# A turned down product in the first MoE, six buffers for the last evictions, and block 0 with whole rows of v

## The chip, the core and the metric

The kernel runs on one core of a Trainium2 chip. Its time is the device time of one execution, in microseconds (us), and smaller is better. Four engines matter: TensorE (PE, with PEld for its weight loads), VectorE (DVE), ScalarE (ACT) and SyncE (SP), which issues all transfers; GpSimd (POOL) does little. The engines run their own instruction lists in order and wait for each other through semaphores.

## What is computed

A linear attention, whose heads are put side by side as 512 features of 2304 tokens, and two MLPs of 512 x 2048 x 512 (called MoE) behind it, all in float32:

```python
q_s = softmax(q, axis=-1)            # over the 64 features of a head
k_s = softmax(k, axis=2)             # over the 576 positions of a sequence
kv = np.einsum('bhsd,bhse->bhde', k_s, v)
x = np.einsum('bhsd,bhde->bhse', q_s, kv)     # (4, 8, 576, 64) -> (2304, 512)
h = x @ w_in;  y = softplus(h) @ w_out        # first MoE
h = y @ w2_in; out = elu(h) @ w2_out          # second MoE
```

## The kernel before

Tokens are cut into six blocks of 384 (t = 0 to 5), and two blocks form a pair (p = 0, 1, 2, called pairs 1 to 3). The 2048 features of an MLP are cut into eight quads of 256 (f = 0 to 7). The kernel goes through 48 quads: MoE m, pair p, quad f.

A quad has an **up product** and a **down product**. The up product (`add_up`) makes 256 features for 768 tokens by a Strassen-like scheme of seven products of 6 matmuls each, 128 x 128 weights against 384 columns, into the two PSUM banks of the ring "ha"; sums and the nonlinearity follow on ScalarE and VectorE. Float32 is imitated with three matmuls in the rounded type fp32r: each operand is split into a high part (gh) and a low part (gl), and high x high, high x low and low x high are added. The first two quads of the first pair use plain f32 instead (`direct`).

The down product (`add_down`) adds the quad to six PSUM banks `acc` (half, r), each 128 tokens x 512 features, that stay open for all eight quads of a pair. There, g is the stationary operand (128 tokens) and w_out the moving one (512 columns): 12 steps of 3 matmuls. Steps of the down product of one quad stand between the up products of the next. After the last quad of a pair, `add_store` copies the six banks to SBUF tiles y (a ring of two buffers), alternating between ScalarE and VectorE, and stores them: to DRAM tiles yd in the first MoE, to the output in the second.

The second MoE needs its input with features on the partitions. `add_y` (L522 to L539) loads each yd tile, turns it on TensorE by four 128 x 128 transposes into a bank of "ha" (py, L528), and ScalarE copies it into sx. The load is released five quads ahead of the pair. `add_forms` makes the operands xf from sx.

The attention runs block by block, in head pairs hp. `add_k` loads k and v, finds the maximum of k over positions (L316, a transpose on TensorE, L327, and a spread by TensorE), subtracts it (L342), takes the exponential (L350, ScalarE) and makes k x v with an additional column of ones (pk, L359); the sums' reciprocal (L368, L372) scales it into the block-diagonal kvbd (L379, ScalarE). v is loaded into rows with one free column per 64 features (L309), so in pieces of 256 bytes. `add_q` takes the softmax of q. For the first two head pairs of blocks 0 and 1 the exponential takes each group of 64 columns in an activation of its own, with the maximum as its bias and the sum as its accumulator (L431); elsewhere VectorE subtracts (L437), one activation follows (L443), and VectorE sums (L447). q is transposed (pq, L482), copied (xq, L488), multiplied by kvbd (px, L498) and copied into sx (L511). Only then can the first up product run (L878).

The order of all instructions is computed by the class `Plan`: a list scheduler that has a duration for every step, a due date for the steps of TensorE, and for each engine takes the step that can start and is due first. The attribute `early` moves a group's due dates forward, and a step that opens a tile waits until its ring has a free buffer. What the scheduler gives is the fixed order in which each engine, SyncE's queue included, runs its list.

## Time and profile before

| | us |
|---|---|
| median of 3 runs | 869.89 |
| lowest and highest run | 867.58, 870.22 |
| the profiled execution | 870.18 |
| its span, first to last instruction | 868.4 |
| TensorE busy in it | 838.6 |

A line of the timeline gives the start and the duration of one instruction, or of several in a row (xN) from the first start to the last end; matmuls are pipelined, so the distance of two starts is what one costs, and its duration contains its way through the array. What ended an engine's idle time stands behind "<-". In the names, `acc<-wo_o,gh` means: writes acc, reads wo_o and gh.

### The profile page before, as it was taken

What the parts mean: (1) busy time and instruction counts of PE and PEld (TensorE: products, weight loads), DVE (VectorE), ACT (ScalarE), POOL (GpSimd) and SP (SyncE); (2) the same over time, 40 slices, a digit from 0 to 9 for tenths busy, and PEclk for the clock granted to TensorE, in tenths of its full rate; (3) what the DMA queues carried; (4) which work ended last, traced back from release to release, by engine and by line L of the source; (5) the groups of instructions that cost most, each with busy time, mean ns of one, the idle gap of its engine ahead of it and who ended that gap; (6) DMA issues with size and microseconds to landing.
All of it is one profiled execution on the core that took longest, in us unless ns stands there. A gap on an engine that the chain in (4) does not pass through costs nothing.

```text
span 868.4 us, 11687 instructions
## 1 busy us (share of the span) xinstructions
PE 838.6 (97%) x4570; PEld 724.9 (83%) x4570; DVE 566.1 (65%) x812; ACT 532.3 (61%) x819; POOL 2.8 (0%) x24
## 2 busy tenths in 40 slices
PE   3889999999999999999999999999999999999996
PEld 2555888888988888988988988899888888888895
DVE  7676887666888779577668677767543446543433
ACT  4777788675686877665566665666534455534433
POOL 0000000000000000000000000000000000000000
PEclk9799999999999999999999999999999999999999
DMA  9868675514987627667664777784664563663521
GB/s 247 241 186 271 236 263 192 146 74 157 279 289 239 212 102 246 242 240 268 236 215 192 284 279 289 281 288 185 218 244 168 190 254 138 237 235 135 208 107 73
DMA packets 66774, 186.35 MB, mean 215 GB/s; under 512 B 22688, under 2 KB 28832, under 8 KB 57760
## 3 DMA queue, kind: packets, MB, share of 16 engines
q1 hardware_dynamic: 66720, 185.61, 61.8%
q8 instruction: 36, 0.59, 0.3%
q14 instruction: 18, 0.15, 0.1%
HBM read 131.07 MB, written 54.53 MB: 214 GB/s over the span
## 4 chain that ended last, share of the span: by engine, by line
PE 88%; ACT 6%; DVE 3%; DMA 1%; issue 1%; SPq 0%; ACTq 0%; DVEq 0%
PE acc L1008 42%; PE ub L817 19%; PE uc L817 9%; PE up L899 5%; PE ua L817 5%; PE acc L1003 2%; PE px L498 2%; PE up L878 1%; ACT q L431 1%; PE py L528 1%; ACT L920 1%; PE pk L359 1%; ACT raw_i L628 1%; DMA k<-in_k_dram 1%; PE pq L482 1%
## 5 line engine op out<-in xcount | busy, mean ns | idle before, releaser
L1008 PE MATMUL acc<-wo_o,gh 128*128 128x512 f32 x1104 | 350.3, 398 | 0.0
L1008 PEld LDWEIGHTS acc<-wo_o,gh 128*128 128x128 f32 x1104 | 201.0, 188 | 28.1 <-issue 0.5
L1008 PE MATMUL acc<-wo_o,gl 128*128 128x512 f32 x552 | 218.5, 396 | 0.1
L817 PE MATMUL ub<-xf,wf_i 128*128 128x384 f32 x960 | 194.9, 337 | 0.0
L817 PEld LDWEIGHTS ub<-xf,wf_i 128*128 128x128 f32 x960 | 172.0, 188 | 13.8 <-ACT s L830 0.6
L851 DVE TENSOR_TENSOR h<-uc,s 128x384 f32<-128x384 f32 x80 | 44.4, 555 | 141.2 <-PE uc L817 129.7
L830 ACT COPY s<-ub 128x384 f32<-128x384 f32 x120 | 57.4, 478 | 111.4 <-PE ub L817 111.1
L1008 PEld LDWEIGHTS acc<-wo_o,gl 128*128 128x128 f32 x552 | 103.4, 187 | 22.8 <-DVE gl L973 0.5
L973 DVE TENSOR_TENSOR gl<-g,gh 128x768 fp32r<-128x768 f32 x92 | 87.8, 954 | 26.5 <-ACT gh L969 26.3
L969 ACT CAST gh<-g 128x768 fp32r<-128x768 f32 x92 | 76.9, 836 | 37.5 <-DVE g L960 36.7
L817 PE MATMUL uc<-xf,wf_i 128*128 128x384 f32 x480 | 97.5, 337 | 0.2 <-ACT g L920 0.2
L817 PEld LDWEIGHTS uc<-xf,wf_i 128*128 128x128 f32 x480 | 85.7, 188 | 7.3 <-DVE h L851 0.9
L899 PE MATMUL up<-xf,wp 128*128 128x384 f32 x288 | 57.0, 344 | 0.9 <-ACT g L920 0.9
L899 PEld LDWEIGHTS up<-xf,wp 128*128 128x128 f32 x288 | 50.5, 188 | 6.4 <-issue 2.1
L817 PE MATMUL ua<-xf,wf_i 128*128 128x384 f32 x240 | 48.2, 335 | 0.1
L960 DVE SCALAR_TENSOR_TENSOR g<-h,u 128x768 f32<-128x768 f32 x48 | 45.9, 956 | 1.2
L817 PEld LDWEIGHTS ua<-xf,wf_i 128*128 128x128 f32 x240 | 42.5, 188 | 0.9 <-DVE h L851 0.6
L948 ACT ACTIVATE u<-h 128x768 f32<-128x768 f32 x48 | 40.6, 845 | 3.8 <-DVE h L851 2.4
L952 ACT ACTIVATE u<-u 128x768 f32<-128x768 f32 x48 | 40.6, 847 | 1.2
L836 ACT COPY h<-ub 128x384 f32<-128x384 f32 x24 | 11.5, 480 | 44.5 <-PE ub L817 44.5
L956 DVE TENSOR_SCALAR u<-u 128x768 f32<-128x768 f32 x48 | 26.7, 555 | 16.3 <-ACT u L952 16.2
L733 ACT CAST wf_i<-r_i 128x512 fp32r<-128x512 f32 (+1 forms) x48 | 23.7, 511 | 17.6 <-PE uc L817 16.6
(90 smaller groups left out, 907.3 us busy)
## 6 DMA issues: line engine op xcount, KB each, us to landing
wo_o<-wod SPq DMA_DIRECT2D x30, 1024.0 KB, 6.8
wf_i<-wfd SPq DMA_DIRECT2D x16, 1792.0 KB, 7.3
raw_i<-in_moe_w_in_dram SPq DMA_DIRECT2D x16, 1024.0 KB, 6.5
raw_o<-in_moe_w_out_dram SPq DMA_DIRECT2D x16, 1024.0 KB, 5.9
wod<-wo_o SPq DMA_DIRECT2D x16, 1024.0 KB, 5.9
wfd<-wf_i SPq DMA_DIRECT2D x8, 1792.0 KB, 9.1
r_i<-w32i SPq DMA_DIRECT2D x24, 512.0 KB, 4.5
w32i<-ti_i SPq DMA_DIRECT2D x14, 512.0 KB, 5.0
```

What stands on the lines that cost most here:

```text
L733: nc.scalar.copy(view(0, lo, n, c), get())
L817: nc.tensor.matmul(ps[:, :BLK], T[wk][:, lo : lo + P], T[xk][:, (2 * c + kc) * BLK : (2 * c + kc + 1) * BLK], start=(i in first and kc == ...
L830: nc.scalar.copy(new(sk), T[key][:, :BLK])
L851: nc.vector.tensor_tensor(T[hk][:, half * BLK : (half + 1) * BLK], T[key][:, :BLK], T[sk], op=ALU.add)
L899: nc.tensor.matmul(ps[:, :BLK], T[wk[a]][:, lo : lo + P], T[xk][:, (2 * c + kc) * BLK : (2 * c + kc + 1) * BLK], start=(n_ == 0 and kc == ...
L948: nc.scalar.activation(new(uk), T[hk], AF.Relu, scale=-1.0)
L952: nc.scalar.activation(T[uk], T[uk], AF.Exp, scale=-1.0)
L956: nc.vector.tensor_scalar(T[uk], T[uk], -1.0, None, op0=ALU.add)
L960: nc.vector.scalar_tensor_tensor(new(gk), T[hk], 0.0, T[uk], op0=ALU.max, op1=ALU.add)
L969: nc.scalar.copy(new(hk), T[gk])
L973: nc.vector.tensor_tensor(new(lk), T[gk], T[hk].bitcast(F32), op=ALU.subtract)
L1008: nc.tensor.matmul(ps, T[g][:, col : col + P], T[wk][:, (2 * a + j) * DM : (2 * a + j + 1) * DM], start=(first and n == 0), stop=(f == NQ ...
```

## The change

1. In the first MoE the down product of pairs 2 and 3 is **turned** (`turned(m, p)`, `add_down_turned`): w_out is now the stationary operand (128 features) and g the moving one (768 tokens). The 768 tokens don't fit a bank of 512 columns, so for each of four groups of features (kc) the first 512 tokens go to a bank of their own, and the last 256 of two groups share a bank: six banks as before. A quad has 8 steps of 6 matmuls, alternating between 512 and 256 columns. `add_store` evicts these six banks and stores them in a DRAM tile with features on the partitions, and `add_y` loads a block of it straight into sx; transposes and copies out of PSUM remain for pair 1 alone.
2. The six evictions at the very end use three rings (y, yl, raw), two buffers each, and get due dates one after the other; the last tile is evicted in two halves, by VectorE and ScalarE.
3. In block 0 each head pair's v is loaded as whole rows of 2304 bytes into a staging tile vr, and ScalarE copies it into v; kvbd is made by VectorE. The activations of 64 columns (L431) are gone; blocks 0 and 1 go the way of the others.
4. The scheduler starts with ScalarE's table set "exp" as loaded, takes TensorE's early steps as 1.1 instead of 2.2 times as long, and has other values of `early`.

```diff
-        lock, table = 0.0, None
+        lock, table = 0.0, "exp"
...
-                dur *= 2.2
+                dur *= PE_EARLY
...
+PE_EARLY = 1.1
...
-        @step(DMA, n * t_dma(2 * P * C * D * 4), w=[vk], after=LAT)
-        def _():
-            for g, hp in enumerate(hps):
-                nc.sync.dma_start(
-                    out=vt()[:, g, :, :D],
-                    in_=v[b, 2 * hp : 2 * hp + 2].rearrange("h (p c) d -> (h p) c d", c=C),
-                )
+        vsrc = lambda hp: v[b, 2 * hp : 2 * hp + 2].rearrange("h (p c) d -> (h p) c d", c=C)
+        if early:
+            vr = ("vr", b, hps[0])
+            @step(DMA, t_dma(P * C * D * 4), make=[(vr, "xf")], after=LAT, behind=[kload[b, hps[0]]])
+            def _():
+                T[vr] = new(vr, F32)[:, : C * D].rearrange("p (c d) -> p c d", c=C)
+                nc.sync.dma_start(out=T[vr], in_=vsrc(hps[0]))
+            @step(ACT, t_act(C * D), r=[vr], w=[vk])
+            def _():
+                nc.scalar.copy(vt()[:, 0, :, :D], T[vr])
...
-        @step(ACT, 0.5 * n, r=[pk, rs], w=[("kvbd", b % 2, hp) for hp in hps])
+        eng = DVE if early else ACT
+        @step(eng, (0.28 if early else 0.5) * n, r=[pk, rs], w=[("kvbd", b % 2, hp) for hp in hps])
         def _():
             for g, hp in enumerate(hps):
                 for j in range(2):
                     rows = slice(64 * j, 64 * j + 64)
-                    nc.scalar.activation(
-                        kvbd[b % 2, hp][rows, rows], pkv()[rows, g, :D], AF.Copy, scale=T[rs][rows, g : g + 1]
-                    )
+                    o, i, f = kvbd[b % 2, hp][rows, rows], pkv()[rows, g, :D], T[rs][rows, g : g + 1]
+                    if eng == DVE:
+                        nc.vector.tensor_scalar(o, i, f, None, op0=ALU.mult)
+                    else:
+                        nc.scalar.activation(o, i, AF.Copy, scale=f)
...
-        if t < 2 and hps[0] < 2:
-            @step(DVE, 0.072, w=[qm])
-            def _():
-                nc.vector.tensor_scalar(T[qm][:, :N], T[qm][:, :N], -1.0, None, op0=ALU.mult)
-            @step(ACT, N * 0.24, r=[qm], w=[qk], make=[(qd, "qd")], tab="exp")
-            def _():
-                new(qd)
-                for j in range(N):
-                    nc.scalar.activation(
-                        flat()[:, j], flat()[:, j], AF.Exp, bias=T[qm][:, j], accum_out=T[qd][:, j]
-                    )
...
+        @step(DVE, t_dve(n), r=[qm], w=[qk])
+        def _():
+            nc.vector.tensor_tensor(
+                flat(), flat(), T[qm][:, :N].to_broadcast([P, N, D]), op=ALU.subtract
+            )
+        @step(ACT, t_act(n), w=[qk], tab="exp")
+        def _():
+            nc.scalar.activation(flat(), flat(), AF.Exp)
+        @step(DVE, t_dve(n), r=[qk], make=[(qd, "qd")])
+        def _():
+            nc.vector.tensor_reduce(new(qd)[:, :N], flat(), axis=AX.X, op=ALU.add)
...
+        if turned(0, t // 2):
+            p, lo = t // 2, t % 2 * BLK
+            @step(
+                DMA, t_dma(P * KC * BLK * 4), r=[("ytd", p, i) for i in range(2 * R)], make=[(xk, "sx")],
+                w=[("xs", 1, t, kc) for kc in range(KC)], after=LAT, behind=behind,
+            )
+            def _():
+                nc.sync.dma_start(
+                    out=new(xk).rearrange("p (k c) -> p k c", k=KC),
+                    in_=T["yd", p].rearrange("p (k c) -> p k c", k=KC)[:, :, lo : lo + BLK],
+                )
+            return
...
+    turned = lambda m, p: m == 0 and p > 0
+    def add_down_turned(m, p, f, wk, t0):
+        for n, (j, kc) in enumerate((j, kc) for j in range(2) for kc in range(KC)):
+            hk, lk = ("gh", m, p, f, j), ("gl", m, p, f, j)
+            keys = [("acc", m, p, kc), ("acc", m, p, KC + kc // 2)]
+            first = f == 0 and j == 0
+            made = keys[: 1 if kc % 2 else 2] if first else []
+            @step(
+                PE, 1.5 * DN, w=[key for key in keys if key not in made], r=[hk, lk, ("woh", m, f), ("wol", m, f)],
+                hold=[wk], make=[(key, f"acc{kc // 2}") for key in made], due=t0 + (2 + n) * UP + 1.5 * n * DN + 0.01,
+                line=("acc", kc),
+            )
+            def _(j=j, kc=kc, hk=hk, lk=lk, keys=keys, made=made, first=first):
+                for key in made:
+                    new(key)
+                parts = [
+                    (T[keys[0]], slice(0, 512), True),
+                    (T[keys[1]][:, kc % 2 * 256 : kc % 2 * 256 + 256], slice(512, 2 * BLK), kc % 2 == 0),
+                ]
+                for n, (g, a) in enumerate(((hk, 0), (hk, 1), (lk, 0))):
+                    lo = (2 * a + j) * DM + kc * P
+                    for ps, cols, starts in parts:
+                        nc.tensor.matmul(
+                            ps, T[wk][:, lo : lo + P], T[g][:, cols],
+                            start=(first and n == 0 and starts), stop=(f == NQ - 1 and j == 1 and n == 2),
+                            skip_group_check=True,
+                        )
...
+        if turned(m, p):
+            return add_down_turned(m, p, f, wk, t0)
...
+        if turned(m, p):
+            T["yd", p] = dp.tile([P, KC * 2 * BLK], F32, name=f"yd{p}")
+            to = T["yd", p].rearrange("p (k c) -> p k c", k=KC)
+            for i, n in enumerate((0, 4, 1, 2, 5, 3)):
+                ak, sk = ("acc", m, p, n), ("yt", m, p, n)
+                eng = DVE if i % 2 else ACT
+                @step(eng, t_act(DM, True) if eng == ACT else t_dve(DM), r=[ak], make=[(sk, "y")], due=after_quad(m, p, NQ - 1) + SLOT)
+                def _(eng=eng, ak=ak, sk=sk):
+                    (nc.scalar.copy if eng == ACT else nc.vector.tensor_copy)(new(sk), T[ak])
+                @step(DMA, t_dma(P * DM * 4), r=[sk], w=[("ytd", p, n)], after=LAT)
+                def _(n=n, sk=sk):
+                    if n < KC:
+                        nc.sync.dma_start(out=to[:, n, :512], in_=T[sk])
+                    else:
+                        lo = 2 * (n - KC)
+                        nc.sync.dma_start(
+                            out=to[:, lo : lo + 2, 512:], in_=T[sk].rearrange("p (k c) -> p k c", k=2)
+                        )
+            return
...
+                final = (m, p) == (1, NPAIR - 1)
+                ring = ("y", "yl", "raw")[(R * half + r) // 2] if final else "y"
+                both = final and (half, r) == (1, R - 1)
+                for n_, eng in enumerate((DVE, ACT) if both else (eng,)):
+                    n = DM // 2 if both else DM
+                    @step(
+                        eng, t_act(n, True) if eng == ACT else t_dve(n), r=[ak],
+                        w=[("y2", m)] if n_ else [], hold=[sk] if n_ else [], make=[] if n_ else [(sk, ring)],
+                        due=after_quad(m, p, NQ - 1) + SLOT + (R * half + r if final else 0), line="y2" if both else None,
+                    )
+                    def _(eng=eng, ak=ak, sk=sk, n_=n_, n=n):
+                        if not n_:
+                            T[sk] = new(sk, F32)[:, :DM]
+                        cols = slice(n_ * n, n_ * n + n)
+                        (nc.scalar.copy if eng == ACT else nc.vector.tensor_copy)(T[sk][:, cols], T[ak][:, cols])
...
-    ATT = ((70.0, 50.0), (35.0, 20.0))
+    ATT = ((120.0, 50.0), (50.0, 10.0))
...
-        early(6.0 if i else 200.0)
+        early(4.0 if i else 200.0)
...
-        early((180.0, 30.0, 0.0)[min(f, 2)] if plain(m, p) else 10.0)
+        early((150.0, 10.0, 0.0)[min(f, 2)] if plain(m, p) else 8.0)
...
-            early(40.0)
+            early(60.0)
```

What this does to the lists, at three places. **ScalarE in block 0**, before: q's activations of 64 columns (L431) and the products for kvbd (L379).

```order
L431 ACTIVATE q_0_210,qd_0_277<-q_0_210,qm_0_244 128x64 x6
L431 ACTIVATE q_1_224,qd_1_286<-q_1_224,qm_1_246 128x64 x6
L350 ACTIVATE k_3_174<-k_3_174 128x576
L443 ACTIVATE q_2_200<-q_2_200 128x384
L443 ACTIVATE q_3_204<-q_3_204 128x384
L379 ACTIVATE kvbd_0_145<-pk_0_258,rs_0_325 64x64 x2
L379 ACTIVATE kvbd_1_146<-pk_1_301,rs_1_365 64x64 x2
L379 ACTIVATE kvbd_2_147<-pk_2_343,rs_2_394 64x64 x2
```

The same stretch of ScalarE now (L445 the exponential of q, L318 the copy of v from vr, L490 the copy of q after its transpose):

```order
L445 ACTIVATE q_0_202<-q_0_202 128x384
L318 COPY v_0_172<-vr_0_233 128x9x64
L445 ACTIVATE q_1_206<-q_1_206 128x384
L445 ACTIVATE q_2_212<-q_2_212 128x384
L445 ACTIVATE q_3_227<-q_3_227 128x384
L318 COPY v_1_175<-vr_1_241 128x9x64
L318 COPY v_2_178<-vr_2_247 128x9x64
L318 COPY v_3_181<-vr_3_254 128x9x64
L490 COPY xq_0_364<-pq_0_365 128x384
```

The short activations and kvbd have left, and four copies of v have come.

**VectorE in block 0**, before: the reciprocals for kvbd (rs), with the maximum of block 1's k (mx, L316) among them.

```order
L368 TENSOR_SCALAR rs_1_365<-pk_1_301 128x1
L372 RECIPROCAL rs_1_365<-rs_1_365 128x1
L316 TENSOR_REDUCE mx_0_370<-k_0_297 128x128
L368 TENSOR_SCALAR rs_2_394<-pk_2_343 128x1
L372 RECIPROCAL rs_2_394<-rs_2_394 128x1
L368 TENSOR_SCALAR rs_3_404<-pk_3_373 128x1
L372 RECIPROCAL rs_3_404<-rs_3_404 128x1
L327 TENSOR_REDUCE m_0_415<-pt_0_413 128x2
```

The same stretch of VectorE now; L394 is kvbd, L652 and L669 make the first weight tile w_ti_i:

```order
L383 RECIPROCAL rs_0_358<-rs_0_358 128x1
L383 RECIPROCAL rs_1_360<-rs_1_360 128x1
L383 RECIPROCAL rs_2_369<-rs_2_369 128x1
L394 TENSOR_SCALAR kvbd_0_145<-pk_0_273,rs_0_358 64x64 x2
L394 TENSOR_SCALAR kvbd_1_146<-pk_1_304,rs_1_360 64x64 x2
L394 TENSOR_SCALAR kvbd_2_147<-pk_2_335,rs_2_369 64x64 x2
L652 SCALAR_TENSOR_TENSOR ti_i_362<-raw_i_184,ti_i_362 128x1024
L327 TENSOR_REDUCE mx_0_408<-k_0_262 128x128
L379 TENSOR_SCALAR rs_3_430<-pk_3_385 128x1
L669 ISA w_ti_i_433<-raw_i_184,ti_i_362 128x2048
```

kvbd for three of four head pairs stands ahead of block 1's maximum, which stood ahead of two of the four reciprocals.

**TensorE at the first down product of pair 2**, before: steps of three matmuls (L1008) among the up products (L817) of the next quad.

```order
L817 MATMUL ua_1_1_1952<-xf_1_2_1428,wf_i_1_1795 128x384 x6
L1008 MATMUL acc_1_0_0_1966<-wo_o_1798,gh_1_0_0_1889 128x512 x2
L1008 MATMUL acc_1_0_0_1966<-wo_o_1798,gl_1_0_0_1896 128x512
L817 MATMUL ub_1_1_1936<-xf_1_6_1693,wf_i_1_1795 128x384 x6
L1008 MATMUL acc_1_0_1_1983<-wo_o_1798,gh_1_0_0_1889 128x512 x2
L1008 MATMUL acc_1_0_1_1983<-wo_o_1798,gl_1_0_0_1896 128x512
L1008 MATMUL acc_1_0_2_1991<-wo_o_1798,gh_1_0_0_1889 128x512 x2
L1008 MATMUL acc_1_0_2_1991<-wo_o_1798,gl_1_0_0_1896 128x512
```

The same place now; L1023 is the turned product, L833 the up product:

```order
L833 MATMUL ua_1_1_1944<-xf_1_2_1464,wf_i_1_1773 128x384 x6
L1023 MATMUL acc_1_0_1954<-gh_1_0_0_1874,wo_o_1793 128x512
L1023 MATMUL acc_1_4_1955<-gh_1_0_0_1874,wo_o_1793 128x256
L1023 MATMUL acc_1_0_1954<-gh_1_0_0_1874,wo_o_1793 128x512
L1023 MATMUL acc_1_4_1955<-gh_1_0_0_1874,wo_o_1793 128x256
L1023 MATMUL acc_1_0_1954<-gl_1_0_0_1878,wo_o_1793 128x512
L1023 MATMUL acc_1_4_1955<-gl_1_0_0_1878,wo_o_1793 128x256
L833 MATMUL ub_1_1_1928<-xf_1_6_1744,wf_i_1_1773 128x384 x6
L1023 MATMUL acc_1_1_1978<-gh_1_0_0_1874,wo_o_1793 128x512
L1023 MATMUL acc_1_4_1955<-gh_1_0_0_1874,wo_o_1793 128x256
```

g has become the moving operand, each weight tile is used for 512 and then for 256 columns, and the first step opens two banks.

## Rows read from the trace of the kernel before

**Rows 1.** The page: busy time and share of each engine, instructions.
```profile
PE 838.6 (97%) x4570; PEld 724.9 (83%) x4570; DVE 566.1 (65%) x812; ACT 532.3 (61%) x819; POOL 2.8 (0%) x24
```

**Rows 2.** Busy time by stretch: length, engines, TensorE's granted clock, DMA share, GB/s.
```profile
0.00:50.00 50.00, 29.22 (x293) 20.78 (x294) 35.56 (x66) 33.83 (x92) 2.23 (x20) 0.88 0.78 220
50.00:110.00 60.00, 59.71 (x286) 39.73 (x285) 45.64 (x53) 41.25 (x53) 0.13 (x1) 0.99 0.77 246
110.00:850.00 740.00, 737.98 (x3943) 654.97 (x3942) 478.37 (x686) 452.11 (x668) 0.39 (x3) 1.00 0.61 215
850.00:868.40 18.40, 11.71 (x53) 9.45 (x51) 6.54 (x9) 5.12 (x7) 0.00 (x0) 0.96 0.23 86
```

**Rows 3.** Timeline of TensorE, 545 to 573: start, duration, instruction, idle before.
```profile
545.96 0.63 PE L1008 MATMUL acc<-wo_o,gh 128*128 128x512 f32 x2
...
548.72 1.23 PE L817 MATMUL ub<-xf,wf_i 128*128 128x384 f32 x6
549.79 1.20 PE L817 MATMUL ua<-xf,wf_i 128*128 128x384 f32 x6
550.83 0.63 PE L1008 MATMUL acc<-wo_o,gh 128*128 128x512 f32 x2
...
571.41 0.60 PE L528 MATMUL py<-ident,yl 128*128 128x128 f32 x4
...
572.54 1.23 PE L817 MATMUL ub<-xf,wf_i 128*128 128x384 f32 x6
```

**Rows 4.** Weight loads by line and form: busy us, mean ns, idle before.
```profile
L817 PEld LDWEIGHTS ub<-xf,wf_i 128*128 128x128 f32 x960 | 172.0, 188 | 13.8 <-ACT s L830 0.6
...
L359 PEld LDWEIGHTS pk<-v,k 64*64 64x64 f32 x576 | 18.8, 142 | 11.1 <-issue 7.0 <-ACT kvbd L379 4.0
```

**Rows 5.** Timeline of the weight loads, 61 to 63 us.
```profile
61.08 2.18 PEld L359 LDWEIGHTS pk<-v,k 64*64 64x64 f32 x72 [0.76 <-issue]
```

**Rows 6.** Instructions of L528: count, ns minimum/median/maximum, first and last start.
```profile
L528 PE MATMUL py<-ident,yl x72: 270/272/277, 443.3 to 717.4; 128*128 128x128 f32 x72
```

**Rows 7.** DMA issues from 850: count, KB each, median us to landing.
```profile
out_dram<-y SPq DMA_DIRECT2D x6, 256.0 KB, 2.0
```

**Rows 8.** Timeline of the end, 861 to 866 us.
```profile
861.32 0.39 PE L1008 MATMUL acc<-wo_o,gl 128*128 128x512 f32 x1
...
861.96 0.58 ACT L1023 COPY y<-acc 128x512 f32<-128x512 f32 x1 [0.25 <-DMA out_dram<-y]
...
863.88 1.53 DVE L1023 COPY y<-acc 128x512 f32<-128x512 f32 x2 [4.16 <-DMA out_dram<-y]
```

**Rows 9.** Chain that ended last, in order of time: start, us, what.
```profile
15.72 3.85 ACT q L431 x23
...
80.72 2.58 PE up L878 x8
```

**Rows 10.** Timeline of blocks 0 and 1, 0 to 53 us.
```profile
0.73 1.81 SPq L294 DMA_DIRECT2D k<-in_k_dram  x4
...
5.93 8.01 SPq L309 DMA_DIRECT2D v<-in_v_dram  x4
...
14.34 1.02 DVE L437 TENSOR_TENSOR q<-q,qm 128x384 f32<-128x384 f32 x2
...
19.47 0.67 ACT L350 ACTIVATE k<-k 128x576 f32<-128x576 f32 x1
...
22.10 0.63 ACT L379 ACTIVATE kvbd<-pk,rs 64x64 f32<-64x64 f32 x2 [1.14 <-DVE qd L452]
...
45.75 1.23 DVE L653 CUSTOM_DVE_ANT_0 w_ti_i<-raw_i,ti_i 128x2048 uint16<-128x2048 uint16 x1
...
46.91 2.11 PE L498 MATMUL px<-xq,kvbd 128*128 128x192 f32 x8 [2.40 <-ACT xq L488]
...
48.81 3.93 PE L878 MATMUL up<-sx,w_ti_i 128*128 128x384 f32 x8
```

**Rows 11.** Busy time by stretch, 3.70 to 46.98 us (columns as in rows 2).
```profile
3.70:46.98 43.28, 26.20 (x284) 18.28 (x284) 32.87 (x65) 29.94 (x87) 0.13 (x1) 0.88 0.83 232
```

22 lines of the change are left out of this document (6 added, 16 removed).

## The prediction

> **What bounds the kernel now.** I read the share of busy time first [rows 1]: TensorE is busy 97% of the 868.4 us, VectorE 65%, ScalarE 61%. Then the same by stage [rows 2]. Between 110 and 850 us TensorE idles 740.0 - 738.0 = 2.0 us in all, so in that stretch the time is the sum of TensorE's instructions and a shorter wait elsewhere buys nothing. The idle time lies at the ends: 20.8 us of the first 50, and 6.7 us after 850. So each part of the change has one of three prices: instructions taken from or given to TensorE in the middle, the date at which TensorE's first long run begins, and what follows the last matmul.
>
> The profiled execution took 870.18 us, 1.8 us more than its span; the median of the runs is 869.89. I work on the span, keep the 1.8 us, and take 0.3 us off at the end.
>
> **Part 1, the turned down product: matmuls.** Pairs 2 and 3 of the first MoE have 16 quads. Before, a quad has 12 steps of 3 matmuls of 512 columns, 36 x 512 = 18432 columns. Now it has 8 steps of 3 x (512 + 256), 24 x 768 = 18432 columns. The columns are equal; there are 16 x 12 = 192 more matmuls, and 16 x 24 = 384 of them have 256 columns, a length that the trace of before does not show in this form. I price it from the nearest forms [rows 3]. From 545.96 to 548.72 twelve matmuls of 512 columns start: 230 ns each. From 549.79 to 550.83 six of 384 columns: 173 ns each. 230/512 and 173/384 are both 0.45 ns per column, so no fixed cost per matmul is left over, and 256 columns would take 115 ns. Three of 512 and three of 256 are then 1.5 times the old three, and the part costs nothing.
>
> What can spoil this is the weight load ahead of each matmul: a load must fit into the matmul before it, and 115 ns would be the shortest cover in this kernel's steady state. A load of 128 columns is recorded with 188 ns, also ahead of the 384-column matmuls that follow each other every 173 ns [rows 3, 4]. So the record holds more than the time for which the load blocks; the load blocks at most 173 ns. A closer bound comes from the small loads of block 1: 72 loads of 64 columns, recorded with 142 ns each, take 2.18 us in all [rows 4, 5], (2.18 - 0.14)/71 = 29 ns apart, alternately for the two halves of the rows, so 57 ns per half. At least 142 - 57 = 85 ns of a record is latency. If that holds for the wide load too, it blocks at most 188 - 85 = 103 ns, 12 ns under the cover. Bounds of the 256-column matmul: 107 ns (its columns at 2.4 GHz, the level granted in this stretch [rows 2]) and 173 ns; over 384 of them that is -3.1 to +22.3 us. I take 115 ns, zero, because the closest rows on both questions say so; the margin is thin, and it is the main risk.
>
> **Part 1, the transposes that go.** The second MoE reads the first one's result. Before, each of the 18 result tiles is loaded and turned by four transposes on TensorE (72 in all), then copied out of PSUM by ScalarE [rows 6]. For the four blocks of pairs 2 and 3 one load per block fetches the turned result straight into sx: 12 groups, 48 transposes, go. A group's price: from 571.41 to 572.54 there are four transposes and three matmuls of 512 columns, 1.13 - 3 x 0.230 = 0.44 us [rows 3]. All on the bound engine: 12 x 0.44 = **-5.3 us**. ScalarE loses 12 copies and "ha" 12 tenants; with 2.0 us of idle in 740 us that is worth nothing more. The new loads are 768 KB each and are released five quads ahead of their use, under TensorE's work on those quads, so they cost nothing; without that cover each would cost at least the 2.0 us from issue to landing that a 256 KB tile needs [rows 7].
>
> The turned accumulators bring one new constraint. At the first step of a pair two banks are opened at once, and six in four steps, so the six evictions of the pair before must follow sooner. TensorE still has two up products (2 x 1.05 us) between the last old step and the first new one, and a step lasts 1.04 us against an eviction of 0.58 to 0.77 us [rows 8], on two engines. Behind the eviction on ScalarE stand casts and the softplus for the next quad. Bounds: 0 to 1.5 us at each of the three boundaries; I take +0.6 us in all.
>
> **Part 2, the last six evictions.** Before, two buffers serve six output tiles. The last matmul ends at 861.32 + 0.39 = 861.71, but the last two evictions start at 863.88, behind a wait of 4.2 us for an output transfer (2.0 us from issue to landing) to give its buffer back, and end at 865.41; the span ends 2.99 us later [rows 7, 8]. Now all six have their own buffer, and the last tile is split over both engines in halves of 256 columns. No wait for a transfer is left; the last tile is evicted right behind its matmul. A half costs between half of 0.77 and the whole of it; I take 0.4 us, with 0.1 us to start. End: 861.7 + 0.5 + 3.0 = 865.2, **-3.2 us** (-2.8 to -3.2). The six transfers need an issue each on SyncE, 0.45 us by the loads of k [rows 10], and tiles end three matmuls, 0.69 us, apart, so SyncE keeps up.
>
> **Part 3, blocks 0 and 1.** Four things move here, and the list of VectorE decides. Removed from ScalarE: 24 activations of 64 columns for the first two head pairs of block 0 (the chain shows 3.85 us of them), 24 for block 1, and 8 products for kvbd (0.63 us a pair) [rows 9, 10]. Added to ScalarE: two exponentials of 384 columns, one of 768, and four copies of v of 576 columns, by the exponential of that size at most 0.67 us each [rows 10]. Added to VectorE: a subtraction and a sum for two halves of block 0, at 0.51 us each [rows 10] 2.0 us; the same at double width for block 1, 1.9 us; eight products of 64 x 64, between half of ScalarE's 0.31 us and that itself, 1.8 us; less 0.4 us of negations. Sum: +5.3 us of VectorE. On SyncE the four loads of v took 8.01 us to issue in pieces of 256 bytes; the four loads of k, whole rows, took 1.81 [rows 10]. So the loads queued behind (k, v and q of block 1, first weights) start about 6 us earlier.
>
> What TensorE waits for: its first long run starts with the third group of up matmuls (eight in plain f32, the first ones of quad f = 1), before at 48.81, behind the px products at 46.91 (waiting for ScalarE's copies) and the second weight tile, which VectorE finishes at 45.75 + 1.23 = 46.98 [rows 10]. From 3.70 to 46.98 VectorE is busy 32.87 of 43.28 us [rows 11]. The new list up to that tile holds the same work and the 5.3 us: without any idle time it ends at 3.7 + 32.9 + 5.3 = 41.9. It can't be without, since maxima go through TensorE and exponentials through ScalarE and back; I allow 2.6 us, a quarter of the 10.4 us that it idles there before, and the tile is ready at 44.5. The px products come before it, since ScalarE's list ahead of those copies is shorter by most of the short activations. So the third up group starts near 45, **-4.0 us**; bounds 0 (VectorE as idle as before, no gain at all) and -6.5. From there TensorE is busy without gaps before (59.7 of 60 us) [rows 2]; VectorE, 45.6 of 60 us there, has room. The shifted dates for attention, forms and weights change the order but no work: I take 0, bounds +-1.5 us.
>
> **Sum.** -5.3 - 3.2 - 4.0 + 0.6 = -11.9 us; 870.2 - 11.9 - 0.3 = **858.0 us**.
>
> **The rivals.**
> 1. *The weight load sticks out (ends slower).* Place: behind each of the 384 matmuls of 256 columns. For it: the record of 188 ns, and no matmul before gives less than 173 ns of cover in this form. Against it: the small loads, and transposes that pass their loads every 109 ns or faster. Price: at 173 ns, 384 x 58 ns = +22.3 us, which gives 880. It turns the sign from 115 + 11.9/0.384 = 146 ns on. Chance 8% for slower; 9% for a part of it (120 to 146 ns, 860 to 870).
> 2. *A fixed cost on each matmul.* Four transposes of 128 columns cost 440 ns, 110 each, where 0.45 ns per column gives 58: were the other 52 ns a fixed cost, the 192 additional matmuls would cost 10.0 us, 868. Against it: plain f32, which the transposes are, has its own pace: eight matmuls of 384 columns hold the chain for 2.58 us [rows 9], 0.84 ns per column, and 128 columns at that pace are 107 ns with next to nothing fixed. Chance 4%. The Trainium skill (TensorEngine Tiling (Array Packing), section "Instruction Overhead") speaks against this change: it gives every matmul an overhead of some 60 cycles. At 2.4 GHz that would be an estimate of 25 ns, 4.8 us for 192, and 863 by it; its chance is within the 4%. By that rule 512 columns would be cheaper per column than 384, and the two equal paces [rows 3] disagree.
> 3. *VectorE eats the early gain.* The +5.3 us are all waited for: no gain in part 3, and 862. For it: VectorE's list is already the longer one there, 32.9 us against 29.9 of ScalarE [rows 11]. Against it: 10.4 us of its idle time. With a wait at each boundary 866. Chance 9%.
>
> **How the numbers follow.** Forecast with its own spread (854 to 861): 70%. Rival 1: 17%, rival 2: 4%, rival 3: 9%. What a measurement of this kernel can tell from no change is 0.3%, 2.6 us. Slower is rival 1 in full, 8%; the same is the upper end of its milder form and of rivals 2 and 3, 7%; faster 85%. The range reaches down to 853 (part 3 and the 256-column matmul both at their low bounds give 852.4) and up to 866, over rival 3 and half of the milder rival 1.
>
> **What would show it.** Step by step: the starts of a turned step's matmuls alternate 230 and 115 ns, a triple pair 1.04 us; if the short one is followed by more than 120 ns, rival 1 or 2. py has 24 transposes instead of 72. After the last matmul 3.5 us remain. The third up group starts near 45 us. No wait of TensorE for a y copy at the three boundaries. The forecast is wrong above all if the 256-column matmuls are not paced by their columns.

## The result, and the profile after

The changed kernel takes **848.9 us** (median; 848.5 to 850.0), the kernel before 870.1 us beside it: ratio 0.9765, 95% interval 0.9744 to 0.9785. The forecast was 858.0 with a range of 853 to 866: the direction was right, but the gain of 21.2 us stands against a forecast of 11.9, and the time lies outside the range, on its fast side. The profiled execution has a span of 847.0 us.

Busy time by stretch after the change, columns as in [rows 2] (length, then TensorE, its weight loads, VectorE, ScalarE, GpSimd, TensorE's granted clock, DMA share, GB/s):

```profile
0.00:50.00 50.00, 32.98 (x319) 21.88 (x320) 44.17 (x82) 30.38 (x48) 2.23 (x20) 1.00 0.82 251
50.00:110.00 60.00, 60.00 (x305) 43.19 (x304) 46.30 (x53) 45.09 (x59) 0.13 (x1) 1.00 0.77 263
110.00:828.60 718.60, 718.25 (x4028) 649.95 (x4028) 468.85 (x678) 436.80 (x645) 0.39 (x3) 1.00 0.61 218
828.60:847.00 18.40, 14.51 (x67) 11.99 (x65) 7.78 (x11) 7.13 (x10) 0.00 (x0) 0.95 0.23 86
```

In the middle TensorE idles 0.35 us (2.0 before), so the time is still the sum of its work. In the first 50 us VectorE went from 35.6 to 44.2 us of work and TensorE's clock from 0.88 to 1.00. TensorE's start, in the timeline (start, duration, instruction, count, idle before):

```profile
15.94 4.89 PE L370 MATMUL pk<-v,k 64*64 64x65 f32 x108 [5.18 <-DVE q L439]
20.77 0.88 PE L484 MATMUL pq<-ident,q 128*128 128x128 f32 x6
22.05 1.26 PE L370 MATMUL pk<-v,k 64*64 64x65 f32 x36 [0.41 <-ACT xq L490]
23.25 1.56 PE L500 MATMUL px<-xq,kvbd 128*128 128x384 f32 x4
...
29.27 2.74 PE L894 MATMUL up<-sx,w_ti_i 128*128 128x384 f32 x8
...
40.97 1.57 PE L500 MATMUL px<-xq,kvbd 128*128 128x192 f32 x8 [0.32 <-ACT xq L490]
42.38 2.74 PE L894 MATMUL up<-sx,w_ti_i 128*128 128x384 f32 x8
```

The third up group starts at 42.38 us (48.81 before [rows 10]; forecast 45), and takes 2.74 us in place of 3.93 (the section on the clock says how far that is a gain). What part 1 and part 2 should show is there. A turned step, and the transposes that are left:

```profile
330.02 0.86 PE L1023 MATMUL acc<-gh,wo_o 128*128 128x512 f32 x4
330.72 0.51 PE L1023 MATMUL acc<-gl,wo_o 128*128 128x512 f32 x2
331.06 0.86 PE L1023 MATMUL acc<-gh,wo_o 128*128 128x512 f32 x4
```

```profile
L544 PE MATMUL py<-ident,yl x24: 270/272/273, 430.9 to 442.9; 128*128 128x128 f32 x24
```

From 330.02 to 331.06 three pairs of 512 and 256 columns take 1.04 us, the forecast's figure; the start after a 512 comes 230 ns later and the one after a 256 comes 117. The 72 transposes [rows 6] are 24. The end of the kernel:

```profile
842.72 0.39 PE L1061 MATMUL acc<-wo_o,gl 128*128 128x512 f32 x1
843.15 0.42 DVE L1112 COPY y<-acc 128x256 f32<-128x256 f32 x1 [0.67 <-PE acc L1061]
843.61 0.37 ACT L1112 COPY y<-acc 128x256 f32<-128x256 f32 x1 [0.55 <-DVE y L1112]
```

No eviction waits for an output transfer any more ([rows 8] has 4.16 us of it). From the last matmul's start to the end there are 847.0 - 842.7 = 4.3 us, where 868.4 - 861.3 = 7.1 stood.

### The profile page after: what moved, and what is told of

Same layout as the page of the kernel before. It is cut to its first block, busy times and chain, and to the rows that moved or that the text cites. A ratio compares the mean times of both kernels' runs of the same rounds, so it can differ in the third digit from the quotient of the medians.

```text
span 847.0 us, 11907 instructions
## 1 busy us (share of the span) xinstructions
PE 825.7 (97%) x4714; PEld 727.0 (86%) x4714; DVE 567.1 (67%) x823; ACT 519.4 (61%) x759; POOL 2.8 (0%) x24
## 4 chain that ended last, share of the span: by engine, by line
PE 91%; DVE 5%; ACT 2%; DMA 1%; issue 1%; SPq 0%; DVEq 0%; ACTq 0%
PE acc L1061 29%; PE ub L833 19%; PE acc L1023 15%; PE uc L833 9%; PE up L915 6%; PE ua L833 5%; PE acc L1056 2%; PE up L894 2%; PE px L500 1%; PE pk L370 1%; PE pq L484 1%; DMA yd<-y 1%; DVE mx L327 1%; DMA k<-in_k_dram 1%; DVE k L353 1%
## 5 line engine op out<-in xcount | busy, mean ns | idle before, releaser
L1061 PE MATMUL acc<-wo_o,gh 128*128 128x512 f32 x720 | 226.3, 395 | 0.0
L833 PE MATMUL ub<-xf,wf_i 128*128 128x384 f32 x960 | 194.6, 337 | 0.0
L833 PEld LDWEIGHTS ub<-xf,wf_i 128*128 128x128 f32 x960 | 167.8, 188 | 11.3 <-ACT s L846 0.5
L1061 PEld LDWEIGHTS acc<-wo_o,gh 128*128 128x128 f32 x720 | 132.2, 188 | 18.6 <-DVE y L1112 0.4
L1061 PE MATMUL acc<-wo_o,gl 128*128 128x512 f32 x360 | 142.5, 396 | 0.0
L1023 PE MATMUL acc<-gh,wo_o 128*128 128x512 f32 (+1 forms) x512 | 112.2, 341 | 0.0
L833 PE MATMUL uc<-xf,wf_i 128*128 128x384 f32 x480 | 97.4, 337 | 0.1
L1023 PEld LDWEIGHTS acc<-gh,wo_o 128*128 128x128 f32 x512 | 83.4, 188 | 7.6 <-issue 0.2
L833 PEld LDWEIGHTS uc<-xf,wf_i 128*128 128x128 f32 x480 | 83.8, 188 | 6.2 <-DVE h L867 0.9
L1061 PEld LDWEIGHTS acc<-wo_o,gl 128*128 128x128 f32 x360 | 67.5, 187 | 14.5
L1023 PE MATMUL acc<-gl,wo_o 128*128 128x512 f32 (+1 forms) x256 | 65.5, 336 | 0.0
L833 PE MATMUL ua<-xf,wf_i 128*128 128x384 f32 x240 | 48.2, 335 | 0.1
L1023 PEld LDWEIGHTS acc<-gl,wo_o 128*128 128x128 f32 x256 | 39.1, 188 | 5.3
L833 PEld LDWEIGHTS ua<-xf,wf_i 128*128 128x128 f32 x240 | 41.7, 188 | 0.9 <-ACT kvbd L396 0.4
```

Of the source, the lines that this page charges most:

```text
L833: nc.tensor.matmul(ps[:, :BLK], T[wk][:, lo : lo + P], T[xk][:, (2 * c + kc) * BLK : (2 * c + kc + 1) * BLK], start=(i in first and kc == ...
L1023: nc.tensor.matmul(ps, T[wk][:, lo : lo + P], T[g][:, cols], start=(first and n == 0 and starts), stop=(f == NQ - 1 and j == 1 and n == 2) ...
L1061: nc.tensor.matmul(ps, T[g][:, col : col + P], T[wk][:, (2 * a + j) * DM : (2 * a + j + 1) * DM], start=(first and n == 0), stop=(f == NQ ...
```

## The experiments

Part 1 and part 2 are items 1 and 2 of the change. Part 3 is, as in the prediction, items 3 and 4 together: the code of blocks 0 and 1, and the scheduler's numbers, here called the constants. Of these, the *factor* is the 1.1 for TensorE's early steps, the *table* is the function table taken as loaded, and the *dates* are ATT and the values of `early`.

The table has for each kernel its median time and ratio to the kernel before (with its 95% interval), and four dates from the profiled execution, read off TensorE's timeline: the third up group; the first up matmul of pair 2; the first of the second MoE; and the start of the last matmul.

| kernel | us | ratio | third up | pair 2 | MoE 2 | last |
|---|---|---|---|---|---|---|
| before | 870.1 | 1 | 48.8 | 200.9 | 470.3 | 861.3 |
| after | 848.9 | 0.9765 (0.9744 to 0.9785) | 42.4 | 189.1 | 456.6 | 842.7 |
| e1 part 3 | 862.8 | 0.9921 (0.990 to 0.994) | 43.0 | 189.7 | 463.8 | 854.4 |
| e2 part 1 | 863.2 | 0.9919 (0.990 to 0.994) | 47.4 | 198.3 | 464.9 | 851.8 |
| e3 part 2 | 866.9 | 0.9964 (0.995 to 0.998) | 48.2 | 199.0 | 468.7 | 859.8 |
| e4 part 3, code | 863.6 | 0.9927 (0.991 to 0.9945) | 44.9 | 194.6 | 464.1 | 855.2 |
| e5 after, old dates | 851.8 | 0.9791 (0.9775 to 0.981) | 43.7 | 192.3 | 459.0 | 845.9 |
| e6 after, old factor | 853.6 | 0.981 (0.979 to 0.983) | 44.8 | 194.2 | 462.6 | 848.5 |
| e7 after, old kvbd | 855.5 | 0.9833 (0.982 to 0.985) | 41.3 | 195.4 | 463.0 | 848.9 |
| e8 after, old v | 853.2 | 0.9813 (0.979 to 0.983) | 42.8 | 192.9 | 460.9 | 846.8 |
| e9 after, old exp | 864.1 | 0.9944 (0.9925 to 0.996) | 50.4 | 204.2 | 471.7 | 857.6 |
| e10 before, filled | 879.2 | 1.0113 (1.009 to 1.0135) | 56.3 | 208.2 | 477.8 | 868.8 |
| e11 128 columns | 890.2 | single run | 44.1 | 190.8 | 495.3 | 884.2 |
| e12 256 columns | 853.6 | single run | 43.5 | 190.2 | 461.3 | 847.6 |
| e13 before, filled 2 | 867.1 | 0.9971 (0.996 to 0.998) | 46.3 | 197.2 | 466.7 | 857.8 |
| e14 part 3, old dates | 861.1 | 0.990 (0.988 to 0.992) | 42.5 | 191.1 | 460.6 | 851.7 |
| e15 after, no constants | 853.4 | 0.981 (0.980 to 0.9825) | 45.1 | 194.7 | 461.3 | 848.1 |
| e16 constants alone | 874.8 | 1.0055 (1.004 to 1.007) | 49.9 | 202.7 | 475.0 | 865.6 |

A date of one execution is good to about 1 us: before, e2 and e3 have the same blocks 0 and 1 and the third up group at 48.8, 47.4 and 48.2; after, e1, e11 and e12 at 42.4, 43.0, 44.1 and 43.5. Their means differ by 4.9 us. The traced execution of e2 is its fastest (860.7, median 863.2), so its dates are early. By the intervals, a difference of two kernels' times is known to some 2 us.

### Each part alone

e1 sets in the changed kernel `turned = lambda m, p: False` and `final = False`; e2 and e3 are the kernel before with part 1 and part 2 added as in the diff; e4 is e1 with the constants back:

```diff
-        lock, table = 0.0, "exp"
+        lock, table = 0.0, None
-PE_EARLY = 1.1
+PE_EARLY = 2.2
-    ATT = ((120.0, 50.0), (50.0, 10.0))
+    ATT = ((70.0, 50.0), (35.0, 20.0))
```

(and the four `early` values). Expected of e1, e2, e3 and e4:

> The kernel before with the whole of part 3 alone (code of blocks 0 and 1 and the scheduler's constants); no turned product, four y buffers as before. Theory A (part 3 was mis-sized, the parts add): everything the changed kernel wins up to pair 2 of the first MoE is won here too: third up group near 42.4 us, pair 2 starts 11 to 12 us earlier, 858.3 us (ratio 0.9865). Rival B (the 2.8 us won during pair 1 come from the turned product's order): only 6.4 + 2.6 = 9.0 us, 861 us (0.990). The forecast's own term of 4.0 us would give 866.

> The kernel before with part 1 alone (turned down product of pairs 2 and 3; old blocks 0 and 1, old constants, old y buffers). Theory A: 0 for the matmuls, 5.3 to 5.9 us for the 12 groups of transposes, up to 0.9 us beside: 863 to 864.5 us (0.993), 256-column matmuls followed by the next after 115 to 117 ns. Rival B (its order also helps pair 1): 860.5 us.

> The kernel before with part 2 alone (six buffers, last tile on two engines). Both theories: 2.8 to 3.2 us less, 867 us (0.9965); first matmul of the last quad at the same date as before, its distance to the end of the span 27.9 us in place of 30.7.

> The kernel before with the code of part 3 alone (v in whole rows, kvbd of block 0 on VectorE, wide exponentials), scheduler constants as before. Theory C (the code carries the early gain): third up group near 42.4 us, TensorE granted 1.00 from 8 to 52 us, 9 us less, 861 us. Rival D (the constants carry it, by the order that they give): third up group at 46 us or later, low granted clock as before between 24 and 36 us, 865 to 867 us.

Part 1 gives 6.7 us (term 4.7) and part 2 gives 2.9 (term 3.2). Part 3 alone reaches pair 2 as early as the changed kernel does, 11.1 us before the kernel before, as theory A has it, but at the end only 7.1 us are left: between pair 2 and the second MoE it takes 274.1 us, e4 269.5. One wait of TensorE makes most of it, in the timeline of e1:

```profile
236.29 1.34 PE L833 MATMUL uc<-xf,wf_i 128*128 128x384 f32 x6
240.74 1.35 PE L833 MATMUL uc<-xf,wf_i 128*128 128x384 f32 x6 [3.11 <-DVE h L867]
```

and on VectorE at that place, where h, which gives uc's bank back, stands behind attention's qd and qn:

```profile
237.73 0.95 DVE L449 TENSOR_REDUCE qd<-q 128x12 f32<-128x768 f32 x1
...
239.19 1.03 DVE L469 TENSOR_TENSOR qn<-q,qd 128x384 f32<-128x384 f32 x2
240.13 0.55 DVE L867 TENSOR_TENSOR h<-uc,s 128x384 f32<-128x384 f32 x1
```

After the wait TensorE's granted clock in e1 is below full for a while (0.50 from 242 to 244 us). In this stage e1 has 3.4 us of idle time on TensorE and e4 has 0.6; that the low clock makes the remaining 1.8 of the 4.6 us is argued from its place:

```profile
235.00:250.00 15.00, 11.89 (x52) 10.02 (x51) 12.90 (x22) 11.71 (x16) 0.00 (x0) 0.89 0.87 291
```

In the changed kernel the turned down product stands here, the planner gives another order, and h runs at 237.02, ahead of qd; the views name no wait of TensorE. e4 lies between its two theories: 6.3 us, 3.9 of them up to the third up group, which starts at 44.9 us.

### Are the constants good by themselves?

e5 puts back only the dates, e6 only the factor and the table (the lines above). e14 is e5's edit in e1, e15 is the changed kernel with all of them back, e16 the kernel before with all the new ones.

> The changed kernel with the dates for attention, forms and weights as before (ATT and the early values); all else changed. TensorE's order is then the same up to the last down steps of quad 2. Theory E (the dates win the 2.8 us of pair 1 by placing attention under longer runs): third up group at 42.4 us as in the changed kernel, but pair 2 of the first MoE starts 2 to 3 us later than 189.1, total 851 to 852 us (1.003). Rival F (the dates are worth nothing, as the forecast had it): pair 2 at 189.1 +- 0.5 us, 848.9 us.

> The changed kernel with the planner's factor 2.2 for TensorE's first 25 us and no function table loaded at its start, as before. Theory D (the order that the planner gives in blocks 0 and 1 carries a part of the early gain): third up group at 44.5 to 45.5 us as with the old constants, pair 2 about 2.5 us later, 851.5 us (1.003). Rival G (only the code counts): 42.4 us and 848.9 us.

> The kernel before with part 3, but the dates as before (code of blocks 0 and 1 and the planner's factor and table alone). If the dates made the wait of 3.1 us for h in pair 2: no such wait, third up group at 43 us, pair 2 at 192 us, 861 to 862 us (0.991), about as much as the whole of part 3 alone. If the wait belongs to the old down product at this point: the wait is there again and the time is 865 us.

> The changed kernel with all of the scheduler's constants as before (factor, table and dates). If code, turned product and buffers add up: 870 - 6.3 - 6.7 - 2.9 = 854 us (0.982), third up group at 45 us, pair 2 at 194.5 us. If the constants are needed to collect the turned product's gain: 857 us or more.

> The kernel before with the scheduler's constants alone (factor, table and dates), old code of blocks 0 and 1, old down product, old y buffers. If the constants bring a gain whatever the code: 5 us less, 865 us (0.994), third up group at 46 us. If they only fit the new code: 870 us or slower.

Without the constants the parts add: 6.3 + 6.7 + 2.9 = 15.9, and e15 wins 16.4. The constants then bring the last 4.5 us of the changed kernel (e15 to after). On the old code the same numbers cost 5.1 us (e16), on the new code without the turned product they bring 0.8 (e4 to e1), no more than the noise. Factor and dates seem to be no sum either: the dates without factor and table bring nothing (e6, 853.6, against e15, 853.4), factor and table without the dates 1.6 (e5), all of them 4.5; the two small figures are within the noise. The traces are sharper. From the third up group to pair 2, e4 and e15 (no new constants) take 149.6 us, e6 (new dates alone) 149.3, e5 and e14 (factor and table alone) 148.6, and the changed kernel, e1, e11 and e12 (all) 146.7. With the factor two matmuls of a down product stand ahead of the third up group instead of behind it, which is most of the step from 149.6 to 148.6; the dates' own place is pair 1, and they need the factor there. Of their 1.9 us, from e5 to the changed kernel, 1.2 are idle time of TensorE; the rest is not explained here. Stretch 110 to 190 of e5, and the only wait of TensorE that the views name there (in the changed kernel there is none in that stretch):

```profile
110.00:190.00 80.00, 78.82 (x513) 67.14 (x512) 56.62 (x73) 58.90 (x84) 0.26 (x2) 1.00 0.49 160
```

```profile
PE up L915 <- ACT g L936: 1.0, 1, 1.0
```

So E holds against F. For e6, D's date came (44.8 us), at about twice D's price. In e14 the wait for h is gone and the time is 861.1: the new dates make that wait, and only beside the old down product. e16 has that wait too, and another one for attention's qn (engine and line, what it waited for: us, times, longest):

```profile
PE uc L846 <- DVE h L880: 3.1, 1, 3.1
PE pq L497 <- DVE qn L482: 2.8, 1, 2.8
```

### The edits of blocks 0 and 1, one undone at a time

```diff
 e7  -        eng = DVE if early else ACT
     +        eng = ACT
 e8  -        if early:
     +        if False:
```

e9 puts the short activations of blocks 0 and 1 back: 12 pairs of an activation and the read of its sum in each (the prediction's 24 counts both).

> The changed kernel with the eight products of kvbd of block 0 back on ScalarE. If VectorE's list alone sets the date of the third up group (1.8 us less on it): 40.6 us and 847 us (0.998). If ScalarE's products hold pk's buffers longer, as before, where TensorE waited 3.9 us for them: third up group at 44 us or later, 850.5 us or more.

> The changed kernel with v of block 0 loaded in pieces of 256 bytes straight to its place, as before; the four copies on ScalarE (2.6 us) go. Theory H (whole rows bring the loads behind them forward and so block 1 and the first weights): the issues take 8 us instead of 4.3, third up group 1.5 to 3.5 us later, 851 us (1.0025). Rival I (loads were not late, VectorE's list decides): 42.4 us, 848.9 us or a little less.

> The changed kernel with the 48 short activations of blocks 0 and 1 back in place of the three wide ones (24 of 64 columns in each block, their negations on VectorE). VectorE's list is 3.9 - 0.4 us shorter, ScalarE's some 5 us longer. Theory J (ScalarE was what held the old start; VectorE's surplus is hidden): third up group 2 to 4 us later, about 45.5 us, 851 to 853 us (1.004). Rival K (VectorE's list decides at all times): third up group 3 us earlier, 846 us.

Each undone edit costs, 6.6, 4.3 and 15.2 us, but together 26, far more than the 10.8 to 11.6 us of the whole part: each run is also a new order, planned with constants that fit the full set, so these are not prices of the edits. What they show is where the loss lies. In e7 the third up group is even 1.1 us earlier, as VectorE's shorter list would have it, and pair 2 starts 6.3 us later, with 2.3 us of TensorE's idle time from 52 to 110 us and 1.2 from 110 to 190, where the changed kernel has none; the rest of the loss stays open. Both theories looked at the wrong place. In e8 the third up group is 0.4 us later and pair 2 3.8, and one wait covers it: TensorE waits 4.2 us for the second tile of w_out's weights. ScalarE's work on that tile had waited for its load, as H has it, though at a place behind the third up group; VectorE's list also has three more steps ahead of the tile's last one:

```profile
46.11 1.15 ACT L644 ACTIVATE raw_o<-raw_o 128x1024 f32<-128x1024 f32 x1 [2.54 <-DMA raw_o<-in_moe_w_out_dram]
54.17 1.70 PE L1056 MATMUL acc<-w_ti_o,g 128*128 128x512 f32 x2 [4.21 <-DVE w_ti_o L669]
```

In e9 the third up group is 8 us behind the changed kernel's, where J had 2 to 4: in block 1 ScalarE holds 12 pairs of activation and read, 0.33 us a pair, from 35.4 to 39.3 us, ahead of kvbd and of the copies that px needs. TensorE waits for one of these copies, and later for VectorE's mx, which stands behind VectorE's own wait for ScalarE:

```profile
40.35 1.26 ACT L396 ACTIVATE kvbd<-pk,rs 64x64 f32<-64x64 f32 x4
42.87 0.86 ACT L503 COPY xq<-pq 128x384 f32<-128x384 f32 x2
43.40 2.73 PE L513 MATMUL px<-xq,kvbd 128*128 128x192 f32 x8 [1.75 <-ACT xq L503]
46.43 0.69 DVE L661 TENSOR_SCALAR ti_o<-raw_o 128x1024 uint32<-128x1024 uint32 x1 [2.22 <-ACT raw_o L657]
49.33 0.44 PE L334 MATMUL pt<-ident,mx 128*128 128x128 f32 x1 [3.19 <-DVE mx L327]
```

TensorE's granted clock falls with these gaps:

```profile
36.00:52.00 16.00, 9.13 (x43) 5.83 (x39) 10.21 (x15) 14.74 (x40) 0.13 (x1) 0.74 0.65 173
```

K falls: VectorE has less to do there, and everything is later.

### What the clock costs

The kernel before, with transposes that nobody reads in TensorE's waits (e10: 83 of them; e13: only the 34 and 13, as shown). `keep_busy(n)` makes n transposes of the identity into a bank taken from the ring "ha"; apart from them the lists of TensorE, VectorE and ScalarE are those of the kernel before:

```diff
+            if t == 0 and hps[0] == 3:
+                keep_busy(34)
...
+                if t == 0 and hp == 0:
+                    keep_busy(13)
```

> The kernel before with TensorE kept busy in its waits of blocks 0 and 1: 83 transposes of the identity into a spare bank (34, 15, 5, 9 and 20, at most 0.11 us each) ahead of the instructions that wait there; nothing reads them. If the low granted clock is a price of its own: clock 1.00 from 24 to 52 us, px of block 0 1.6 us in place of 2.9, third up group 47.5 to 48 us in place of 48.8 and its run 1.2 us shorter, in all 1.5 to 2.5 us less, 868 us (0.998). If the clock costs nothing, since the other engines' lists decide there: 870 us, or 871 where the transposes stand in the way.

> The kernel before with 47 transposes of the identity into a spare bank, 34 ahead of the last pk of block 0 and 13 ahead of its first px, all ended before the up products need the bank. If the low granted clock is a price of its own: clock 1.00 from 24 to 36 us, first up group 1.5 to 2.5 us earlier than 38.4, the third at 47 us, 868 us (0.998). If the other engines decide: dates as before and 870 us. For comparison: the whole of part 3 brought the first up group to 29.3 us, so the clock can carry no more than a fifth of that.

e10 told nothing on its question: its spare bank is one of the two of the up products, and they wait for ScalarE to empty the other:

```profile
PE up L892 <- ACT g L934: 7.9, 2, 5.2
```

e13 gives the bank back in time. The stretch from 24 to 36 us before, and in e13:

```profile
24.00:36.00 12.00, 8.94 (x27) 5.11 (x25) 8.14 (x12) 8.71 (x17) 0.00 (x0) 0.58 0.99 261
```

```profile
24.00:36.00 12.00, 10.12 (x138) 7.39 (x138) 9.16 (x14) 10.14 (x23) 0.00 (x0) 1.00 1.00 261
```

The first px of block 0 and the third up group, before, in e3 (the same blocks without a fill) and in e13:

```profile
28.90 2.93 PE L498 MATMUL px<-xq,kvbd 128*128 128x384 f32 x4 [1.60 <-ACT xq L488]
29.50 2.93 PE L513 MATMUL px<-xq,kvbd 128*128 128x384 f32 x4 [1.58 <-ACT xq L503]
48.24 2.74 PE L907 MATMUL up<-sx,w_ti_i 128*128 128x384 f32 x8
28.85 1.56 PE L508 MATMUL px<-xq,kvbd 128*128 128x384 f32 x4 [0.16 <-ACT xq L496]
46.30 2.74 PE L888 MATMUL up<-sx,w_ti_i 128*128 128x384 f32 x8
```

The four px take 1.56 us instead of 2.93, the third up group comes 2.5 us earlier (1.2 to 1.9 against e2 and e3), and the time is 867.1, **2.6 us** less (interval 1.5 to 3.6): a gain from work that computes nothing. The granted clock is a price of its own. The third up group's 3.93 us before [rows 10], at a granted clock of 0.60 from 48 to 52 us, is a low clock too, but its end can't be put down to the fill: in e2 and e3 the group takes 2.74 us without one. In e4 it is 1.00 in each 4 us from 24 to 52 us without any fill, so up to 2.6 of the 6.3 us of part 3's code may be the clock; that they are the same 2.6 is argued, not shown.

### How thin the cover of a weight load is

e11 cuts each turned matmul of 256 columns in two of 128, e12 each one of 512 in two of 256:

```diff
 e11 -     (T[keys[1]][:, kc % 2 * 256 : kc % 2 * 256 + 256], slice(512, 2 * BLK), kc % 2 == 0),
     +     (T[keys[1]][:, lo_ : lo_ + 128], slice(512, 640), kc % 2 == 0),
     +     (T[keys[1]][:, lo_ + 128 : lo_ + 256], slice(640, 768), False),
```

> The changed kernel with each of the 384 turned matmuls of 256 columns cut in two of 128, each with its weight load: the cover for a load falls from 116 to 58 ns. If a 128-column weight load blocks 103 ns or more (the bound of the prediction): two pieces take 206 ns or more instead of 116, 384 x 90 = 35 us, 884 us. If loads are hidden at any length and columns alone count: 848.9 us.

> The changed kernel with each of the 384 turned matmuls of 512 columns cut in two of 256: 384 more matmuls and weight loads, the columns unchanged. If every matmul had a fixed cost of 25 ns: 9.6 us, 858.5 us. If the pace is that of the columns alone: a triple pair still takes 1.04 us and the time is 848.9 us, to 1 us.

Each was run once, at a granted clock of 1.00. TensorE in e12, then in e11 (three matmuls to a pair now), then e11's two short matmuls behind the 512 of 339.63 (the second one also alone), and its weight loads at the same place:

```profile
330.56 0.88 PE L1024 MATMUL acc<-gh,wo_o 128*128 128x256 f32 x6
331.28 0.52 PE L1024 MATMUL acc<-gl,wo_o 128*128 128x256 f32 x3
```

```profile
339.63 0.62 PE L1025 MATMUL acc<-gh,wo_o 128*128 128x512 f32 x3
340.08 0.61 PE L1025 MATMUL acc<-gl,wo_o 128*128 128x512 f32 x3
```

```profile
339.91 0.33 PE L1025 MATMUL acc<-gh,wo_o 128*128 128x128 f32 x2
339.97 0.28 PE L1025 MATMUL acc<-gh,wo_o 128*128 128x128 f32 x1
```

```profile
339.46 0.41 PEld L1025 LDWEIGHTS acc<-gh,wo_o 128*128 128x128 f32 x3
```

In e12 six matmuls of 256 columns take 331.28 - 330.56 = 0.72 us, 120 ns each. From pair 2 to the fifth quad of the second MoE, ahead of which the last turned step ends, e12 needs 335.1 us and the changed kernel 331.2: 3.9 us for 384 more matmuls, 10 ns each, between its two theories. The Trainium skill (TensorEngine Tiling (Array Packing), section "Instruction Overhead") gives each matmul some 60 cycles; at 2.4 GHz that is an estimate of 25 ns, 9.6 us for 384, and this run doesn't show them. In e11 a 512 and two 128s take 450 ns where a 512 and a 256 take 350; the stretch is 371.2 us, 40 us more, which is 104 ns for each of the 384 cuts. The 512 has a pace of 230 ns, so the two short ones add 450 - 230 = 220 ns, 110 each, where their columns would need 58. The loads have that pace: three start within 0.41 - 0.19 = 0.22 us, 110 ns apart. A fixed cost of 110 ns on each matmul is not what is seen: the two short ones start only 0.06 us apart (339.91, 339.97), and the time lies behind the 512 (0.28 us to the next start) and behind the second short one (0.11). So a weight load costs about 110 ns where it isn't covered. The Trainium skill (TensorE: Matmul & The Clock Gate, section "LDWEIGHTS (loading the stationary operand)") gives columns / 1.2 in ns, 107 for 128 columns, and this run agrees. The forecast's bound was "at most 103": so in the changed kernel the 256-column matmul covers its successor's load with some 6 ns to spare, not 12, and two of them in a row, at 120 ns, may already show a little of it.

## Why the prediction was wrong

- **The step that failed is part 3's term, -4.0 us with bounds 0 and -6.5.** Beside parts 1 and 2 it measured, by difference, 21.2 - 6.7 - 2.9 = 11.6 us; alone (e1) 7.1, because of the wait for h. The 11.6 us are 6.3 of the code (e4) and 4.5 of the constants, with 0.8 left within the noise.
  - *"I take 0" for the shifted dates, bounds +-1.5.* The constants are worth 4.5 us here (e15 to after), three times the bound. They change no work, as the prediction says, but the time in this stretch is not only work: with them the third up group starts at 42.4 us instead of 45.1, and from there to pair 2 it takes 146.7 us instead of 149.6, with 1.2 us less of idle time on TensorE. The sum also had no place for the planner's factor and table, which the dates need to bring anything (e6).
  - *The clock was given no price.* [rows 2] has 0.88 for the first 50 us, and no term of the sum returns it. e13 puts 2.6 us on it in the kernel before. The code's 6.3 us exceed by about as much, 2.4, the 3.9 by which it moves the third up group; that the clock is this excess is argued.
  - *The date of the third up group.* With the code alone it starts at 44.9, as forecast ("near 45"), but by luck, for the forecast's path is not the one that sets it. In e4 the weight tile is ready at 41.58 + 1.23 = 42.81 us; the group stands behind px, and px waits for ScalarE's kvbd of block 1, which waits for VectorE's reciprocal:

```profile
41.58 1.23 DVE L669 CUSTOM_DVE_ANT_0 w_ti_i<-raw_i,ti_i 128x2048 uint16<-128x2048 uint16 x1
43.17 1.29 ACT L396 ACTIVATE kvbd<-pk,rs 64x64 f32<-64x64 f32 x4 [1.13 <-DVE rs L383]
43.85 1.25 PE L500 MATMUL px<-xq,kvbd 128*128 128x192 f32 x6 [1.08 <-ACT kvbd L396]
44.94 2.74 PE L894 MATMUL up<-sx,w_ti_i 128*128 128x384 f32 x8
```

The mean date of the executions with all of part 3 is 43.3, and there, too, the group starts behind px (42.38, with the tile ready at 41.63, in the changed kernel). With the constants the weight tile is ready at 41.63 instead of the forecast's 44.5. Half of that is idle time on VectorE, 1.3 us where 2.6 were allowed; the other half is its work, 36.7 us, which is 3.8 more than the 32.9 before and not 5.3:

```profile
3.70:41.63 37.93, 36.66 (x76) 1.00 0.78 250
```

The loads behind v start some 3 us earlier (block 1's k is issued at 10.88 us; 13.98 before) and not 6: v's four issues as whole rows take 4.33 us, where the forecast went by k's 1.81:

```profile
6.08 4.33 SPq L314 DMA_DIRECT2D vr<-in_v_dram  x4
```

  - "From there TensorE is busy without gaps" looked at 50 to 110 us. Pair 1 goes on to 200, and before, the stretch from 110 to 200 still had 1.1 us of waits, which the new order doesn't have.
- **Part 1's matmuls: right, with some luck.** 115 ns forecast, 117 measured; the 1.04 us step is there. Rival 1 fell, but by less than the prediction thought: its bound of 103 ns for a load was wrong, e11 has 110, and the cover holds by some 6 ns that no row of before showed. Rival 2 fell: 10 ns per added matmul, and in e12 only.
- **Part 1's transposes: right, a little small.** e2 wins 6.7 us where 5.3 - 0.6 = 4.7 were forecast. The 0.6 us at the boundaries did not come: in e2 and the changed kernel the views name no wait of TensorE from 195 to 465 us. From the fifth quad of the second MoE (520.3 us after, 533.0 before) to the last matmul the changed kernel takes 322.5 us and the kernel before 328.3: 5.8 us for 12 groups, 0.49 each rather than 0.44 (0.2 of the 5.8 is idle time before). From pair 2 to that quad the changed kernel takes 331.2 us and the kernel before 332.2: another 1.0 us, 0.3 of it idle time, the rest open.
- **Part 2: right, 0.3 to 0.4 us too large.** The two halves of the last tile do not run side by side: ScalarE's starts at 843.61, behind VectorE's, which is its releaser. The prediction had 0.5 us from the last matmul to the last eviction's end; it is 843.98 - 843.11 = 0.87.
- **Rival 3 fell.** VectorE's surplus was real (36.7 us of work in a shorter stretch than the 32.9 of [rows 11]) and the gain stayed: VectorE idles 1.3 us up to the weight tile where it idled 10.4.
- **The range** took the terms' bounds one by one, but gave the moved order a bound of 1.5 us without a row for it. The rows could not give one: e16 shows that the same numbers can cost 5 us.

## What to carry to other kernels

An order that a planner makes has a price of several microseconds of either sign, which no sum of instructions shows: give it a wide bound, and tune its numbers on the final code, since here they cost 5.1 us on the old code and won 4.5 on the new. Where a stretch's granted clock is below full, price its return as a term of its own, and look at the whole stretch behind a moved date, not at its start alone. Undoing one edit in a planned kernel measures the edit and a new order together; adding parts from the other side (e2, e3 and e4, with e15 as their sum) gave prices that add up, and e1, the constants on the old down product, shows where that ends.
